# Third token tile from the transposed copy of x, its statistics through DRAM; tiles 4 and 5 split one tile sooner

## The chip, the core and the metric

The kernel runs on one core of a Trainium2 chip. The metric is the time on the device in microseconds (us), the median of several runs; lower is better. The engines are PE (matrix multiplication, with PEld for its weight loads), DVE, ACT and POOL (elementwise work, each strictly in the order of its own instruction list) and SP (here only a queue that issues DMAs and waits for semaphores).

## What is computed

One layer over 2048 tokens of width 640, all in float32. With xn the layer norm of x over its last axis:

```
q, k, v = split(xn @ wqkv)                      # 32 heads of 20
phi(u)  = [softmax(u @ w_phi), softmax(-(u @ w_phi))]   # per head, 40 features
kv, z   = sum over tokens of phi(k)^T v, of phi(k)
s       = (phi(q) kv / (phi(q) z + 1e-6)) @ wo
h       = gelu(xn @ w1 + b1);  g = silu(h @ w2 + b2)    # inner width 1536
out     = x + s * g
```

## The kernel before, in words

The tokens are 16 tiles of 128 (t = 0 to 15); two neighbours t = 2q and 2q + 1 make a pair q, with o = t % 2. The host hands over x twice: row by row (`x`) and transposed (`xt_in`). Every matmul in full precision is three matmuls in a faster format: each operand is split into a high part (a copy in that format, on ACT) and a low part (operand minus high part, on DVE or POOL), and `PASSES` (line 386) lists high x high, high x low, low x high.

**Start (to about 12 us).** PE folds w_phi into the key weights (`fold_w`, line 169), which gives `wk_s`, five pieces of 128 rows of the contraction.

**Keys and values, the stage of the change (about 12 to 150 us).** For each tile PE does `project(t, wk_s)` (line 388, 30 matmuls at line 397) and `value(t)` (line 451, 30 more). The keys go through `feat1` (maximum over a head, subtraction, minimum on DVE at lines 409 to 415; then the negative half on POOL, line 416), `feat2` (exponential on ACT, line 425) and `key_fin` (sums over a head and reciprocal on DVE, lines 433 and 465; scaling on POOL, line 438). `kv_pair(t)` (line 483) then adds the products of two tiles to one PSUM bank on PE (line 477); it follows the key projection of every odd tile from t = 3 on and takes tiles t - 3 and t - 2. Results of PE for one tile lie in `bankA`, three PSUM buffers in rotation. For tiles 4 to 7 `fold_pair` (line 180) also prepares query weights in such buffers, read by DVE at lines 187 and 188.

**How a tile of x becomes PE's stationary operand.** Both ways need the normalized x with the contraction on the partitions, split by `plain` (line 268; ACT at line 272, DVE at 274).
- By transposes (tiles 0, 1 and 2): `norm_a` or `stats` (line 215) take mean and variance per token on DVE, POOL raises the variance to the power -1/2 (line 223), DVE or ACT normalizes the tile (`norm_b`, `norm_act`), and `transpose_x` (line 377) does five PE transposes into PSUM, from which `plain` splits.
- From the transposed copy (tile 3 alone, then the pairs from 4 and 5 on): the statistics lie along partitions, but are now wanted along the free axis of all 128 partitions. So mean and power are stored to DRAM (`st_dram`), and a second DMA reads them back for every partition (`bc`). SP issues the store once POOL's power is there (lines 361, 322), and the broadcast when the store has landed (lines 363, 324). POOL then subtracts the mean (`one_sub`, line 370; for a pair `pair_sub`, two instructions at line 331), DVE multiplies (`one_plain`, line 374; `pair_mul`, line 336), and `plain` splits from SBUF. `one_load` (line 342) and `load_xr` (line 248) fetch the transposed x.

**What sets the order.** The whole start stage and the key stage are scheduled by hand: every engine, SP included, runs its instructions in the order in which the program issues them (`startup`, line 542). An instruction that waits holds up all that is behind it on its engine. Buffers for rows of x, raw weights, broadcasts and value rows come from one pool of eleven (`rows`), which is why the loads of tiles 6 and 7 wait on SP for tiles 0 and 1 to be done with. The lines around the change are 546 to 636: on POOL the order there is the low parts of the value weights (`split_v`, line 139), the negative half of tile 1's keys (416), `one_sub(3)` (370), the powers of tiles 4 and 5 (223), the scaling of tiles 0 and 1 (438), and, in the turn of tile 2, its negative half and `pair_sub(2)` (331).

**Pairs and the rest (from about 150 us).** Later tiles are handled in pairs with fewer multiplications by sums and differences of halves; then the feed-forward layers (lines 987 and 1016, about 237 to 550 us) and the attention output with the gate (line 1218, to the end).

Of the kernel before, what the change touches and what calls it, by code (L numbers as in the profile page):

```python
# [46 lines left out]
def hedgehog_gated_mlp_kernel(ctx: ExitStack, tc: tile.TileContext, x, xt_in, wqk, bd, wv, wo, w1, b1, w2, b2, out_t):  # L47
    nc = tc.nc
# [67 lines left out]
    b1t = const.tile([P, NF], F32, name="b1t")  # L116
# [34 lines left out]
    def load_fold(which, engs):  # L151
        tl = folds[:, which]
        for c, eng in enumerate(engs):
            if c == 1 and which:
                x_in(0, nc.scalar)
            eng.dma_start(tl[:, c], wqk[which, c, :, :6 * P].rearrange("p (i t) -> p i t", i=6))
        return tl
# [72 lines left out]
    def norm_a(t):  # L230
        sm = small.tile([P, 16], F32, tag="st", name="st")
        nrm[t] = sm, stats(t, sm, None, sm[:, 14:15])
# [6 lines left out]
    def norm_act(t):  # L239
        sm, xt = nrm.pop(t)  # L240
        nc.vector.tensor_scalar(sm[:, 15:16], sm[:, 12:13], -1.0, sm[:, 14:15], op0=OP.mult, op1=OP.mult)
        nc.scalar.activation(xt[:], xt[:], AF.Identity, bias=sm[:, 15:16], scale=sm[:, 14:15])
        xns[t] = xt
# [4 lines left out]
    def load_xr(q):  # L248
        h, p = divmod(q, SLOTS)
        xr = slab(F32, "xr", (P, KC, W2))[:]  # L250
        src = xt_in.rearrange("(k p) (h o q t) -> p k h o q t", p=P, h=NH, o=2, q=SLOTS)[:, :, h, :, p]
        nc.sync.dma_start(xr[:, :, :P], src[:, :, 0])
        nc.sync.dma_start(xr[:, :, P:], src[:, :, 1])
        xrs[q] = xr
# [13 lines left out]
    def plain(q, o, v, only=slice(0, 2), hi=True, lo=None):  # L268
        parts = [(xp[:, 0:5, :, at(q)], v)] if o == 0 else [(beside(q), v[:, 0:2]), (xp[:, 5:8, :, at(q)], v[:, 2:5])]
        parts = parts[only]  # L270
        for dst, src in parts if hi else ():
            nc.scalar.activation(dst[:, :, 0, :], src, AF.Copy)
        for dst, src in parts if lo is None else ():
            nc.vector.tensor_tensor(dst[:, :, 1, :], src, dst[:, :, 0, :].bitcast(F32), op=OP.subtract)
        for dst, src in parts if lo else ():
            nc.gpsimd.tensor_tensor(dst[:, :, 1, :], src, dst[:, :, 0, :].bitcast(F32), op=OP.subtract)
# [38 lines left out]
    def pair_stats(t):  # L315
        if t % 2 == 0:
            pst[0] = small.tile([P, 2, 2], F32, tag="pst", name="pst")
        sm = small.tile([P, 16], F32, tag="st", name="st")
        stats(t, sm, pst[0][:, t % 2, 0:1], pst[0][:, t % 2, 1:2])
        if t % 2:  # L320
            q = t // 2
            nc.sync.dma_start(st_dram[q].rearrange("i p s -> p i s"), pst[0][:])
            bc = row([P, W2, 2], F32, "bc")
            nc.sync.dma_start(bc[:].rearrange("p t s -> p (t s)"),
                              st_dram[q].rearrange("i p s -> (i p s)").partition_broadcast(P))
            pld[q] = bc

    def pair_sub(q):
        bc, xr = pld[q], xrs[q]
        for o in (slice(0, P), slice(P, W2)):  # L330
            nc.gpsimd.tensor_tensor(xr[:, :, o], xr[:, :, o], bc[:, None, o, 0].to_broadcast([P, KC, P]),
                                    op=OP.subtract)
# [9 lines left out]
    def one_load(t):  # L342
        q = t // 2
        h, p = divmod(q, SLOTS)
        xr = slab(F32, "xr", (P, KC, W2))[:]
        src = xt_in.rearrange("(k p) (h o q t) -> p k h o q t", p=P, h=NH, o=2, q=SLOTS)[:, :, h, t % 2, p]
        nc.sync.dma_start(xr[:, :, :P], src)
        xrs[t, "one"] = xr[:, :, :P]

    def one_stats(t):  # L350
        sm = small.tile([P, 16], F32, tag="st", name="st")
        ps = sm[:, 14:16]
        xt, st = xts.pop(t), sm[:, :12]
        for i in range(2):
            nc.vector.bn_stats(st[:, 6 * i:6 * i + 6], xt[:, i * HALF:(i + 1) * HALF])
        yield
        nc.vector.bn_aggr(sm[:, 12:14], st.rearrange("p (a b) -> p a b", a=2))
        nc.vector.tensor_scalar(ps[:, 1:2], sm[:, 13:14], LN_EPS, None, op0=OP.add)
        nc.gpsimd.tensor_tensor(ps[:, 1:2], ps[:, 1:2], mhalf[:], op=OP.pow)
        nc.vector.tensor_copy(ps[:, 0:1], sm[:, 12:13])  # L360
        nc.sync.dma_start(st_dram[t // 2, t % 2], ps)
        bc = row([P, P, 2], F32, "bc")
        nc.sync.dma_start(bc[:].rearrange("p t s -> p (t s)"),
                          st_dram[t // 2, t % 2].rearrange("p s -> (p s)").partition_broadcast(P))
        pld[t, "one"] = bc
        yield

    def one_sub(t):
        bc, xr = pld[t, "one"], xrs[t, "one"]
        nc.gpsimd.tensor_tensor(xr, xr, bc[:, None, :, 0].to_broadcast([P, KC, P]), op=OP.subtract)  # L370

    def one_plain(t):
        bc, xr = pld.pop((t, "one")), xrs.pop((t, "one"))
        nc.vector.tensor_tensor(xr, xr, bc[:, None, :, 1].to_broadcast([P, KC, P]), op=OP.mult)
        plain(t // 2, t % 2, xr)

    def transpose_x(t):
        q, o = divmod(t, 2)
        xn = xns.pop(t)
        ps = bankA()  # L380
        flat = ps[:].rearrange("p a b -> p (a b)")
        for k in range(KC):
            nc.tensor.transpose(flat[:, k * P:(k + 1) * P], xn[:, k * P:(k + 1) * P], ident[:])  # L383
        plain(q, o, flat[:, :D].rearrange("p (k t) -> p k t", t=P))
# [3 lines left out]
    def project(t, ws, mid=None, at_k=3):  # L388
        q, o = divmod(t, 2)
        ps = bankA()  # L390
        n = 0
        for k in range(KC):
            if k == at_k and mid is not None:
                mid()
            for a, b in PASSES:
                for hf in range(2):
                    nc.tensor.matmul(ps[:, hf, :HALF], stat_x(q, o, k, a),  # L397
                                     ws[k][:, b, hf * HALF:(hf + 1) * HALF],
                                     start=n == 0, stop=n == 3 * KC - 1)
                n += 1  # L400
        return ps
# [22 lines left out]
    def feat2(ef):  # L424
        nc.scalar.activation(ef, ef, AF.Exp)  # L425
        return ef
# [24 lines left out]
    def value(t, mid=None):  # L451
        ps = project(t, wv_s, mid)
        v, v3 = value_row()
        nc.scalar.activation(v3[:, :, :DH].rearrange("p (a h) d -> p a h d", a=2), heads(ps), AF.Copy)
        return v
# [12 lines left out]
    def key_fin(ef):  # L468
        scale_heads(ef, key_sums(ef))
        return ef  # L470
# [62 lines left out]
    def x_in(t, eng=None):  # L533
        xts[t] = load_x(t, eng)
# [13 lines left out]
    wv_raw = [load_raw(wv[c * P:(c + 1) * P, :]) for c in range(KC)]  # L548
    for t in (3, 4, 5):
        x_in(t)  # L550
    x_in(6)
    x_in(7)
    nc.sync.dma_start(b1t[:], b1)
    nc.sync.dma_start(b2t[:], b2)
    wv_s = []

    def split_v(c):
        wv_s.append(split_w(wv_raw[c][:], "wv", "dve" if c == 3 else "pool"))
# [10 lines left out]
    norm_a(1)  # L569
    fold_w(wkT, range(4, KC), "wk", wk_s)  # L570
    norm_act(1)
    norm_a(2)
    st3 = one_stats(3)
    next(st3)
    split_v(0)
    one_load(3)
    kvp[0] = bankB("kv")
    pk = project(0, wk_s, lambda: transpose_x(1), 4)
    split_v(1)
    next(st3)  # L580
    load_xr(2)
    norm_act(2)
    split_v(2)
    es[0] = feat1(pk)
    split_v(3)
    pk = project(1, wk_s, lambda: transpose_x(2))
    split_v(4)
    feat2(es[0])
    es[1] = feat1(pk)
    one_sub(3)  # L590
    pair_stats(4)
    vs[0] = value(0)
    pair_stats(5)
    wqT = load_fold(0, (nc.sync,) * KC)
    x_in(8)
    x_in(9)
# [3 lines left out]
    one_plain(3)  # L600
    phis[0] = key_fin(es.pop(0))
    vs[1] = value(1)
    phis[1] = key_fin(es.pop(1))
    vf = [v_forms(0), v_forms(1)]
    for t in range(2, 6):
        pk = project(t, wk_s)
        if t % 2:
            kv_pair(t - 3)
        es[t] = feat1(pk)
        if t == 4:  # L610
            next(vf[0])
        if t == 2:
            pair_sub(2)
            pair_stats(6)
            pair_stats(7)
            pair_mul(2)
        if t == 3:
            pair_plain(2)
        if t > 3:
            pair_stats(t + 4)  # L620
        if t in (3, 4, 5):
            spill(t - 3)
        if t == 5:
            x_in(10)
        if t == 4:
            pair_sub(3)
            pair_mul(3)
        vs[t] = value(t)
        if t >= 4:
            fold_pair(t - 4)  # L630
        if t == 5:
            next(vf[0])
        feat2(es[t])
        if t == 4:
            pair_plain(3)
        phis[t] = key_fin(es.pop(t))
# [200 lines left out]
    for p in range(5, 8):  # L837
        t = 2 * p
# [781 lines left out]
```

## Time and profile before

| what | value |
|---|---|
| median of 3 runs | 639.14 us (639.01 to 639.66) |
| the profiled execution | 637.78 us |
| its span, first to last instruction | 636.1 us |
| PE busy | 631.3 us, 99% |
| POOL busy | 432.5 us, 68% |
| DVE busy | 511.1 us, 80% |
| granted PE clock | 1.0 |

All rows come from the one profiled execution. In a timeline a row reads: start in us from the span's start, duration, engine, line, operation, output<-inputs, shape, count, and in brackets how long the engine sat idle before it and what ended that. Durations of neighbouring PE rows overlap; what a step takes is seen from one start to the next. A row of waits reads: who <- whom: us in total, times, longest. A row of a window reads: from:to, length, then busy us and count of PE, PEld, DVE, ACT and POOL, granted clock, share of the DMA engines, GB/s.

### The profile page before, as it was taken

The page shows a single profiled execution, that of the slowest core. Times are in us where ns is not written, and L with a number is a line of the kernel's source. Part 1 is how long each engine was busy: PE and PEld are TensorE (multiplying, and loading weights), DVE is VectorE, ACT ScalarE, POOL GpSimd, SP SyncE. Part 2 cuts the span into 40 slices and gives each one's busy share as a digit, 9 for nine tenths or more (in the row PEclk, how much of TensorE's full clock was granted, in tenths as well). Part 3 has the DMA queues.
Part 4 walks back from the last instruction along what each step waited for, and adds up shares of the span by engine and source line. Part 5 has one row for each costly group of instructions (what it writes and reads, how often), then busy time and mean ns, then how long its engine had stood idle before and what let it go on. Part 6 is the DMA issues. An engine that isn't in the chain of part 4 may idle for free.

```text
span 636.1 us, 11441 instructions
## 1 busy us (share of the span) xinstructions
PE 631.3 (99%) x4324; PEld 550.3 (87%) x4324; DVE 511.1 (80%) x790; ACT 259.7 (41%) x390; POOL 432.5 (68%) x376
## 2 busy tenths in 40 slices
PE   9999999999999999999999999999999999999997
PEld 9999999999999998888888888888888888667676
DVE  5887976789887877878979869758798899887586
ACT  3522422334344347243442534842322335455540
POOL 1877466888978857687878876381735678866363
PEclk9999999999999999999999999999999999999999
DMA  9577287393421488359899699697498598969934
GB/s 347 121 227 230 75 286 223 100 344 134 90 76 42 131 304 284 111 106 349 212 287 315 162 385 350 135 319 258 138 245 168 172 176 271 306 181 310 377 110 152
DMA packets 167168, 136.90 MB, mean 215 GB/s; under 512 B 89864, under 2 KB 130824, under 8 KB 166728
## 3 DMA queue, kind: packets, MB, share of 16 engines
q1 hardware_dynamic: 164376, 124.56, 65.9%
q10 hardware_dynamic: 2736, 11.60, 4.7%
q8 instruction: 34, 0.56, 0.4%
q14 instruction: 22, 0.18, 0.1%
HBM read 87.76 MB, written 48.38 MB: 214 GB/s over the span
## 4 chain that ended last, share of the span: by engine, by line
PE 98%; DMA 1%; DVE 0%; SPq 0%; issue 0%
PE pB L1016 26%; PE pB L987 23%; PE pA L397 22%; PE pB L1218 10%; PE pA L710 7%; PE pB L1144 3%; PE pA L164 2%; PE qV L710 2%; PE kv L477 2%; PE qY L710 1%; DMA folds<-in_wqk_dram 1%; PE pB L1126 0%; PE pA L383 0%; DVE y L1228 0%; PE pB L942 0%; DVE xres L1229 0%
## 5 line engine op out<-in xcount | busy, mean ns | idle before, releaser
L1016 PE MATMUL pB<-hs,w2s 128*128 128x512 f32 x720 | 165.9, 389 | 0.0
L1016 PEld LDWEIGHTS pB<-hs,w2s 128*128 128x128 f32 x720 | 135.0, 188 | 28.8 <-issue 0.8
L987 PE MATMUL pB<-xp,w1s 128*128 128x512 f32 x324 | 81.4, 389 | 0.0
L987 PE MATMUL pB<-xd,w1s 128*128 128x512 f32 x324 | 79.3, 389 | 0.0
L438 POOL TENSOR_TENSOR eq<-eq,rc 128x1280 f32<-128x1280 f32 x16 | 37.9, 2371 | 60.6 <-DVE rc L1078 48.4
L987 PEld LDWEIGHTS pB<-xp,w1s 128*128 128x128 f32 x324 | 60.7, 188 | 12.8 <-ACT x L1003 0.3
L987 PEld LDWEIGHTS pB<-xd,w1s 128*128 128x128 f32 x324 | 60.8, 188 | 12.6
L1025 DVE TENSOR_TENSOR y<-pB,y 128x512 f32<-128x512 f32 x100 | 63.1, 675 | 1.8 <-PE pB L1016 1.8
L992 ACT ACTIVATE pB<-pB,b1t 128x512 f32<-128x512 f32 x48 | 31.8, 662 | 77.3 <-DVE pB L1418 29.5
L397 PE MATMUL pA<-wk,xp 128*128 128x320 f32 x384 | 59.6, 310 | 0.0
L425 ACT ACTIVATE e<-e 128x1280 f32<-128x1280 f32 x32 | 40.7, 1271 | 43.3 <-POOL e L416 42.8
L397 PEld LDWEIGHTS pA<-wk,xp 128*128 128x128 f32 x384 | 56.9, 188 | 0.1
L416 POOL TENSOR_TENSOR e<-nr,e 128x640 f32<-128x640 f32 x32 | 44.8, 1402 | 15.9 <-DVE nr L415 15.5
L438 POOL TENSOR_TENSOR e<-e,rc 128x1280 f32<-128x1280 f32 x16 | 38.4, 2407 | 21.0 <-DVE rc L465 21.0
L1065 POOL TENSOR_TENSOR ez<-eq,zrep 128x1280 f32<-128x1280 f32 x16 | 47.4, 2962 | 2.8 <-DMA eq<-e_dram 2.8
L505 POOL TENSOR_TENSOR w1s<-raw,w1s 128x640 fp32r<-128x640 f32 (+1 forms) x18 | 25.4, 1410 | 18.0 <-ACT w1s L504 17.7
L139 POOL TENSOR_TENSOR w2s<-raw,w2s 128x640 fp32r<-128x640 f32 x23 | 36.1, 1589 | 0.2 <-ACT w2s L137 0.2
L998 DVE TENSOR_TENSOR hs<-pB,hs 128x512 fp32r<-128x512 f32 x48 | 32.0, 683 | 3.8 <-ACT hs L994 3.6
L137 ACT ACTIVATE w2s<-raw 128x640 fp32r<-128x640 f32 x24 | 17.2, 735 | 41.5 <-DVE dn L433 12.1
L409 DVE TENSOR_REDUCE mx<-pA 128x32 f32<-128x640 f32 x32 | 25.9, 809 | 8.9 <-PE pA L397 8.6
L994 ACT ACTIVATE hs<-pB 128x512 fp32r<-128x512 f32 x48 | 28.8, 600 | 2.1
L397 PE MATMUL pA<-wq,xp 128*128 128x320 f32 x192 | 29.6, 309 | 0.0
(220 smaller groups left out, 1281.0 us busy)
## 6 DMA issues: line engine op xcount, KB each, us to landing
raw<-in_w_dram SPq DMA_DIRECT2D x42, 320.0 KB
e_dram<-e ACTq DMA_DIRECT2D x16, 640.0 KB
eq<-e_dram SPq DMA_DIRECT2D x16, 640.0 KB
phi_t<-eq SPq DMA_DIRECT2D x64, 160.0 KB
phT<-phi_t SPq DMA_DIRECT2D x20, 512.0 KB
xt<-in_x_dram SPq DMA_DIRECT2D x16, 320.0 KB
xres<-in_xt_dram SPq DMA_DIRECT2D x20, 256.0 KB
out_dram<-xres SPq DMA_DIRECT2D x19, 256.0 KB
```

The lines of the kernel that those rows point to most:

```text
L139: eng.tensor_tensor(sl[:, 1, :], raw, sl[:, 0, :].bitcast(F32), op=OP.subtract)
L397: nc.tensor.matmul(ps[:, hf, :HALF], stat_x(q, o, k, a), ws[k][:, b, hf * HALF:(hf + 1) * HALF], start=n == 0, stop=n == 3 * KC - 1)
L416: rest = lambda: nc.gpsimd.tensor_tensor(e5[:, :, :, 1, :], nr[:, :, :, None].to_broadcast([P, 2, 16, DH]), e5[:, :, :, 0, :], op=OP.subtract)
L425: nc.scalar.activation(ef, ef, AF.Exp)
L438: nc.gpsimd.tensor_tensor(e3, e3, rc[:, :, None].to_broadcast([P, 64, DH]), op=OP.mult)
L710: nc.tensor.matmul(bank[ch], q_x(blk, a, q), p_weight(base, f, w, k)[:, b], start=ch not in seen and n == 0, stop=n == len(mms) - 1, skip_ ...
L987: nc.tensor.matmul(bank[ch][:], tl[:, a, off + wo_:off + wo_ + P], mov(blk, b), start=new and n == 0, stop=n == len(mms) - 1, skip_group_c ...
L998: nc.vector.tensor_tensor(hs[:, 1], ps, hs[:, 0].bitcast(F32), op=OP.subtract)
L1016: nc.tensor.matmul(ps[:], ws[i][:, b, d * P:(d + 1) * P], hs[o][i][:, a, :], start=i == n == 0, stop=(i, n) == (GF - 1, 2), skip_group_che ...
L1025: nc.vector.tensor_tensor(y, ps[:], y, op=OP.add)
L1065: nc.gpsimd.tensor_tensor(zv, ef, zf, op=OP.mult)
L1218: nc.tensor.matmul(ps[:, mv], w, o[:, mv], start=first and n == 0, stop=last and n == len(steps) - 1, skip_group_check=True)
```

## The change

Tile 2 leaves the way by transposes and takes tile 3's. `one_stats(2)` stores its statistics and broadcasts them (directly ahead of the first half of `one_stats(3)`), `one_load(2)` fetches its transposed x (ahead of the rows of tiles 6 and 7), `one_sub(2)` stands on POOL between the last value weights and the negative half of tile 1's keys, `one_mul(2)` on DVE between the statistics of tiles 4 and 5. `norm_act(2)`, and `transpose_x(2)` within the key projection of tile 1, are gone. The two bias loads move behind tile 3's broadcast on SP. For the pair of tiles 4 and 5, `pair_sub(2)` moves ahead of `key_fin` of tile 1 on POOL, and `pair_plain(2)` from the turn of tile 3 to that of tile 2.

```diff
--- before.py
+++ after.py
@@ -369,10 +369,13 @@
         bc, xr = pld[t, "one"], xrs[t, "one"]
         nc.gpsimd.tensor_tensor(xr, xr, bc[:, None, :, 0].to_broadcast([P, KC, P]), op=OP.subtract)
 
-    def one_plain(t):
+    def one_mul(t):
         bc, xr = pld.pop((t, "one")), xrs.pop((t, "one"))
         nc.vector.tensor_tensor(xr, xr, bc[:, None, :, 1].to_broadcast([P, KC, P]), op=OP.mult)
-        plain(t // 2, t % 2, xr)
+        return xr
+
+    def one_plain(t):
+        plain(t // 2, t % 2, one_mul(t))
 
     def transpose_x(t):
         q, o = divmod(t, 2)
@@ -548,10 +551,9 @@
     wv_raw = [load_raw(wv[c * P:(c + 1) * P, :]) for c in range(KC)]
     for t in (3, 4, 5):
         x_in(t)
+    one_load(2)
     x_in(6)
     x_in(7)
-    nc.sync.dma_start(b1t[:], b1)
-    nc.sync.dma_start(b2t[:], b2)
     wv_s = []
 
     def split_v(c):
@@ -569,28 +571,34 @@
     norm_a(1)
     fold_w(wkT, range(4, KC), "wk", wk_s)
     norm_act(1)
-    norm_a(2)
+    for _ in one_stats(2):
+        pass
     st3 = one_stats(3)
     next(st3)
+    one_load(3)
     split_v(0)
-    one_load(3)
     kvp[0] = bankB("kv")
     pk = project(0, wk_s, lambda: transpose_x(1), 4)
     split_v(1)
     next(st3)
+    nc.sync.dma_start(b1t[:], b1)
+    nc.sync.dma_start(b2t[:], b2)
     load_xr(2)
-    norm_act(2)
     split_v(2)
     es[0] = feat1(pk)
     split_v(3)
-    pk = project(1, wk_s, lambda: transpose_x(2))
+    pk = project(1, wk_s)
     split_v(4)
+    one_sub(2)
     feat2(es[0])
     es[1] = feat1(pk)
     one_sub(3)
     pair_stats(4)
+    x2 = one_mul(2)
     vs[0] = value(0)
+    plain(1, 0, x2, lo=False)
     pair_stats(5)
+    plain(1, 0, x2, hi=False)
     wqT = load_fold(0, (nc.sync,) * KC)
     x_in(8)
     x_in(9)
@@ -600,6 +608,7 @@
     one_plain(3)
     phis[0] = key_fin(es.pop(0))
     vs[1] = value(1)
+    pair_sub(2)
     phis[1] = key_fin(es.pop(1))
     vf = [v_forms(0), v_forms(1)]
     for t in range(2, 6):
@@ -610,11 +619,9 @@
         if t == 4:
             next(vf[0])
         if t == 2:
-            pair_sub(2)
             pair_stats(6)
             pair_stats(7)
             pair_mul(2)
-        if t == 3:
             pair_plain(2)
         if t > 3:
             pair_stats(t + 4)
```

## Prediction

> **What bounds the kernel now.** I read the page first: engines, then the chain that ended last.
>
> ```profile
> PE 631.3 (99%) x4324; PEld 550.3 (87%) x4324; DVE 511.1 (80%) x790; ACT 259.7 (41%) x390; POOL 432.5 (68%) x376
> PE 98%; DMA 1%; DVE 0%; SPq 0%; issue 0%
> PE pA L541 <- PEq L1610: 0.8, 1, 0.8
> PE pA L164 <- DMA folds<-in_wqk_dram: 0.2, 1, 0.2
> ```
>
> The last two lines are the whole list of waits of the PE. After 7.9 us it waits for nothing until its last matmul. So an instruction taken from the PE is worth its slot, and any new wait of the PE, however early, is added in full, since no later idle time can take it back. The question is how much cover each input of the PE has. I read that from the timelines of PE, SP and POOL up to 70 us.
>
> **What is taken from the PE.** The timeline of the PE around the five transposes of tile 2 and the steps behind them:
>
> ```profile
> 20.49 0.71 PE L383 MATMUL pA<-ident,xt 128*128 128x128 f32 x5
> 20.95 2.00 PE L397 MATMUL pA<-wk,xp 128*128 128x320 f32 x12
> 22.79 4.56 PE L397 MATMUL pA<-wv,xp 128*128 128x320 f32 x30
> 27.19 1.92 PE L397 MATMUL pA<-wv,b 128*128 128x320 f32 x12
> 31.59 4.56 PE L397 MATMUL pA<-wk,xp 128*128 128x320 f32 x30
> 44.88 1.37 PE L477 MATMUL kv<-e,v 128*32 128x40 f32 x128
> 46.19 2.02 PE L397 MATMUL pA<-wv,b 128*128 128x320 f32 x12
> 66.65 1.39 PE L477 MATMUL kv<-e,v 128*32 128x40 f32 x128
> 67.97 2.02 PE L397 MATMUL pA<-wv,b 128*128 128x320 f32 x12
> L383 PE MATMUL pA<-ident,xt x15: 270/272/328, 10.6 to 20.9; 128*128 128x128 f32 x15
> ```
>
> Undisturbed, 30 projection matmuls take 27.19 - 22.79 = 4.40 us, 0.147 each. The transposes take 20.95 - 20.49 = 0.46 us from start to start, and the 12 matmuls behind them 1.84 instead of 1.76, so 0.08 for the change of kind. The removal is worth 0.54 us, and everything behind it on the PE is due 0.54 us earlier: the projection of tile 2 at 31.05, the kv products of tiles 0 and 1 at 44.34 and, half of 46.19 - 44.88 later, those of tile 1 at 45.0 (before 45.54).
>
> The mean of one transpose in the last row, 272 ns, would give 1.36 us, but the transposes overlap. The Trainium skill (TensorE: Matmul & The Clock Gate, Part 4: PE-mode transpose) gives about 275 ns for a transpose in one kernel's context; five would give 1.4 us, and the sum would come out 0.8 us lower. The trace agrees with the duration and not with its use as a price.
>
> ACT loses one normalization and two copies' work of tile 2 becomes a copy from SBUF; DVE gains a multiplication. Neither engine sets an end here, except as said below.
>
> **What is added: a round trip through DRAM, ahead of another one.** Tile 3 makes this trip already, and tiles 4 and 5 a second one. SP's and POOL's timelines have all their steps:
>
> ```profile
> 9.21 8.20 SPq L132 DMA_DIRECT2D xt<-in_x_dram  x5
> 20.77 0.34 SPq L361 DMA_DIRECT2D st_dram<-st  x1
> 23.94 0.33 SPq L363 DMA_DIRECT2D bc<-st_dram  x1
> 24.32 0.43 SPq L252 DMA_DIRECT2D xr<-in_xt_dram  x1
> 31.69 0.37 SPq L322 DMA_DIRECT2D st_dram<-pst  x1
> 34.94 0.34 SPq L324 DMA_DIRECT2D bc<-st_dram  x1
> 35.33 2.86 SPq L156 DMA_DIRECT2D folds<-in_wqk_dram  x5
> 16.61 0.55 POOL L223 TENSOR_TENSOR st<-st,mhalf 128x1 f32<-128x1 f32 x1 [1.62 <-DVE st L222]
> 24.25 1.57 POOL L139 TENSOR_TENSOR wv<-raw,wv 128x640 fp32r<-128x640 f32 x1
> 26.41 1.28 POOL L416 TENSOR_TENSOR e<-nr,e 128x640 f32<-128x640 f32 x1 [0.59 <-DVE nr L415]
> 28.80 1.59 POOL L370 TENSOR_TENSOR xr<-xr,bc 128x640 f32<-128x640 f32 x1 [1.12 <-DMA bc<-st_dram]
> 37.28 2.37 POOL L438 TENSOR_TENSOR e<-e,rc 128x1280 f32<-128x1280 f32 x1
> 40.84 3.15 POOL L331 TENSOR_TENSOR xr<-xr,bc 128x640 f32<-128x640 f32 x2
> ```
>
> SP stands still between a store of statistics and the broadcast that reads it: 23.94 - 20.77 = 3.17 us, and 34.94 - 31.69 = 3.25 for the pair. From the issue of a 128 KB broadcast to POOL's use of it pass 28.80 - 23.94 = 4.86 us. In the new order SP issues store 2, broadcast 2, the xr load of tile 3, store 3, broadcast 3, and only then the loads of pair 2; the pair's store waits for POOL, and POOL's list has the subtraction of tile 3 ahead of the pair's statistics.
>
> Is the second trip served beside the first, or behind it? Three rows, the first the rate in 40 slices from 24.3 to 30.5 us, the others windows (the last column is GB/s):
>
> ```profile
> GB/s 0 0 0 0 0 40 7 26 33 0 0 0 0 0 0 0 0 79 132 99 109 145 182 215 264 317 344 340 353 353 340 340 291 268 221 221 211 241 59 0
> 34.90:39.10 4.20, 4.20 (x31) 4.20 (x30) 4.10 (x6) 0.00 (x0) 4.20 (x4) 1.00 0.50 60
> 39.10:45.00 5.90, 5.90 (x52) 5.71 (x55) 3.33 (x11) 1.87 (x2) 5.90 (x6) 1.00 1.02 407
> ```
>
> First bytes come 1.1 us after the broadcast's issue, then almost none until 26.9, though 640 KB of xr loads stood issued behind it from 24.32 on. Over 34.90 to 39.10 move 60 x 4.2 = 252 KB, which is the pair's 256 KB broadcast alone, while fold loads issued from 35.33 wait. So a broadcast holds up what is queued behind it, for about 4.2 us from its issue. The Trainium skill (DMA: Bandwidth & Descriptors, Queues, rings and completion order) says the same: an engine consumes the descriptors of one ring in order.
>
> Now the sum in absolute times. Store 2 is ready when POOL's power ends (17.16) and SP is past the fifth x load (17.41), so 17.45; 320 KB of that load, 0.8 us at 407 GB/s, stand ahead of it, so its wait is 3.2 to 4.2, I take 4.0. **T = 21.4** (20.4 to 21.7) for broadcast 2.
> Tile 2: subtraction on POOL at T + 4.86 = 26.3, when POOL is through with the last wv part (before: 25.8), until 27.9; the exponent's partner of tile 1 (L416) follows until 29.2, before it ended at 27.7.
> Tile 3: its store, issued at T + 0.85, moves when broadcast 2 and the 320 KB load (at the 340 GB/s of the first row) have passed, T + 4.2 + 1.0; behind the bytes lies 3.2 - 1.1 = 2.1. Broadcast 3 goes at T + 7.3 = 28.7 (T + 4.05 if nothing queues), and the subtraction of tile 3 starts at 28.7 + 4.86 = **33.6** instead of 28.80.
> Pair 2: from that subtraction to the pair's store were 31.69 - 28.80 = 2.89 us, so the store goes at 36.5, the broadcast at 39.7, and it is there at 39.7 + 4.86 to 5.4 (it has twice the bytes; I take 5.2) = 44.9. Its subtractions take 3.1 us, to 48.0.
> The change puts these subtractions ahead of the scaling of tile 1's features (L438) on POOL; that scaling takes 2.37 and ends at **50.4**. Before, it ended at 39.65, and its cover until the PE used it was 45.5 - 39.65 = 5.9 us. The PE wants it at 45.0, so it stands still for **5.4 us**.
>
> **What is late next.** Behind the stall PE and POOL start together, at E = 50.4. In the trace of before the PE takes 67.97 - 45.54 = 22.4 us from the kv products of tile 1 to the values of tile 5, which take over a PSUM bank that DVE's folded-query work (L188) must have read.
>
> ```profile
> 45.43 1.48 DVE L433 TENSOR_REDUCE rc<-e 128x64 f32<-128x1280 f32 x1
> 49.81 0.89 DVE L274 TENSOR_TENSOR xp<-xr,xp 128x640 fp32r<-128x640 f32 x1
> 51.87 1.27 ACT L425 ACTIVATE e<-e 128x1280 f32<-128x1280 f32 x1 [0.28 <-POOL e L416]
> 53.17 1.49 DVE L433 TENSOR_REDUCE rc<-e 128x64 f32<-128x1280 f32 x1 [0.59 <-ACT e L425]
> 66.86 0.49 DVE L188 TENSOR_TENSOR sr<-sr,pA 128x320 f32<-128x320 f32 x1
> 30.43 0.82 DVE L374 TENSOR_TENSOR xr<-xr,bc 128x640 f32<-128x640 f32 x1 [1.53 <-POOL xr L370]
> 45.55 0.74 ACT L272 ACTIVATE xp<-xr 128x640 fp32r<-128x640 f32 x1 [3.09 <-DVE xr L336]
> 0.84 4.18 PE L541 MATMUL pA<-const-float32-1.0 128*128 128x128 f32 x18 [0.84 <-PEq L1610]
> ```
>
> The other side of that bank: L416 and the exponent of tile 2 (1.28 + 1.27), sums and features (49.81 - 45.43 = 4.38), the same pair for tile 3 (2.55) make E + 9.5, and from the sums of tile 3 to the read of the bank were 67.35 - 53.17 = 14.2: E + 23.5 or so. That is **1.0 us** of a second wait.
> The split of tile 4, in the L274 row, was ready at 50.70, when the PE began tile 4 (50.68); the change takes it to 50.4 to 51.2, five microseconds ahead of the delayed use, so it gains nothing. The split of tile 2 gets ready at about 31.0: POOL to 27.9, the L374 kind 0.82, one statistics block of the pair on DVE ahead of the low half (about 1.3, beside ACT's 0.74), an L274 kind of 0.89. It is used at 31.05; were it late by some tenths, the stall at 45 would swallow that.
> The last row is a clock term: the first 18 matmuls of the kernel, after an idle PE, take 4.18 us, 0.22 apart, against 0.09 for transposes of the same shape. If 5.4 us of idle bring that state back, four microseconds at half rate cost up to 2.0 us, of which the second wait swallows 1.0. From nothing to 1.0; I take 0.5. The Trainium skill (TensorE: Matmul & The Clock Gate, Part 1) puts the loss of the clock at an idle window of some 3.4 us; by it the term would be full. No wait of that length stands in this trace.
>
> **Sum:** -0.54 + 5.4 + 1.0 + 0.5 = +6.4 us. The profiled execution has 637.78 us (span 636.1 and 1.7 around it), so 644.2 for one like it; it lies 1.36 below the median of the runs, 639.14, from which I forecast **645.5**.
>
> **Rivals.**
> *Trips side by side* (0.15). If store 3 does not queue, tile 3's subtraction starts at T + 4.05 + 4.86, 29.3 to 30.6, and the scaling ends 16.8 later, at 46.1 to 47.4: stalls of 1.1 to 2.4 and of 1.0, less 0.54, +1.6 to +2.9, which is 640.7 to 642.0. Against it speak the rate rows above.
> *No stall* (0.13). If the trips are so short that the scaling of tile 1 ends by 45.0, 5.4 us sooner than in my sum, only the gain is left: -0.54, 638.6. It is the one that decides the other way, from the point where the pair's broadcast is there by 39.5. For it: the cover of 5.9 us, and three stores and three broadcasts in a row in which an error adds up. Against it: a store took 3.17 and 3.25, a broadcast 4.86 on a queue with nothing ahead. The Trainium skill (DMA: Bandwidth & Descriptors, Anatomy of one DMA) has about 2 us plus the bytes at 436 GB/s; by it store and broadcast would take 2.0 and 2.3 us and this rival would hold. The trace differs on both.
> *Longer* (0.07). A third late resource, such as later wq folds behind the later broadcast of the pair, takes it past +8.5.
> The forecast has 0.65. Its own range: T from 20.4 to 21.7, broadcast of the pair 4.86 to 5.4, clock term 0 to 1.0: +4.5 to +7.4, and with 1 us more on the second wait +8.4.
>
> A measurement of this kernel tells about 0.2% (1.3 us) from no change. Faster by more than that needs over twice the removed PE time: 0.03. The no-stall case falls within: 0.13. The rest, 0.84, is slower. The range runs from the side-by-side case to the forecast's upper end: 640.4 to 647.6.
>
> **What would show it.** Waits of the PE: a new line at L477 on POOL of about 5.4 us, and one of about 1 us at L397 on DVE near 75 us. POOL: L370 twice, the second near 33.6 waiting for the broadcast, and L331 near 45 waiting likewise, ahead of a L438. SP: two waits of 3 to 7 us at L363. Right in kind but not in size, if L477 waits 1 to 2 us. Wrong, if L477 does not wait, or if the PE waits first for tile 2's split.

## The result, and the profile after

The changed kernel takes 648.99 us (median of 4 runs, 648.88 to 651.01), the kernel before 639.18 us beside it (639.01 to 639.66): a ratio of 1.0161, 95% interval 1.0146 to 1.0176. It is 9.8 us slower. The prediction had slower, by 6.4 us, and the time lies above its range. The profiled execution is the longest of the four (651.01 us, span 649.3); of the others there is no trace. The lines of the changed file are 3 higher than before from `project` on: 397 has become 400, 416 is 419, 425 is 428, 433 is 436, 438 is 441, 477 is 480; in some of the runs below a line stands a little further on (L401 or L421 for L400, L442 for L441, L718 for L717). One run of all, 708.65 us at a granted clock of 0.85, in the first filling of the long wait, is left out of the numbers below.

First the page's engine line and its chain of work that ended last, then the list of the PE's waits (without those of the first microseconds and one of 0.2):

```profile
PE 633.7 (98%) x4319; PEld 551.8 (85%) x4319; DVE 516.7 (80%) x791; ACT 259.2 (40%) x389; POOL 434.3 (67%) x377
PE 74%; POOL 7%; DVE 7%; DMA 6%; issue 2%; ACT 1%; SPq 1%; ACTq 0%; POOLq 0%; DVEq 0%
```

```profile
PE kv L480 <- POOL e L441: 6.1, 1, 6.1
PE pA L717 <- DVE e L415: 1.7, 1, 1.7
PE pA L400 <- ACT xp L272: 1.4, 1, 1.4
...
PE pA L717 <- DVE v L731: 0.8, 1, 0.8
```

The chain that was 98% PE now runs through the other engines for a quarter of the span: up to the last of these waits the PE no longer sets the pace. The timeline of the PE shows where it falls behind:

```profile
44.86 0.80 PE L480 MATMUL kv<-e,v 128*32 128x40 f32 x64
51.74 1.29 PE L480 MATMUL kv<-e,v 128*32 128x40 f32 x64 [6.08 <-POOL e L441]
52.96 3.36 PE L400 MATMUL pA<-wv,b 128*128 128x320 f32 x12
74.76 1.39 PE L480 MATMUL kv<-e,v 128*32 128x40 f32 x128
77.55 2.00 PE L400 MATMUL pA<-wv,b 128*128 128x320 f32 x12 [1.40 <-ACT xp L272]
161.76 1.12 PE L717 MATMUL pA<-wv,xp 128*128 128x320 f32 x6 [1.72 <-DVE e L415]
```

Against the rows of before (44.88, 66.65, 67.97, and 45.54 for the second half of the kv products) the PE is level at 44.86, 6.2 us late at 51.74, 8.1 late at 74.76 and 9.6 late at 77.55. The rest of the 13.2 us between the spans, 3.6, falls behind that. "Level" hides a gain: this execution began its folds 0.4 us later.

Now the way of the statistics, on SP and on POOL:

```profile
17.62 0.33 SPq L361 DMA_DIRECT2D st_dram<-st  x1
21.84 0.33 SPq L363 DMA_DIRECT2D bc<-st_dram  x1
...
22.75 0.46 SPq L361 DMA_DIRECT2D st_dram<-st  x1
29.00 0.32 SPq L363 DMA_DIRECT2D bc<-st_dram  x1
...
37.06 0.37 SPq L322 DMA_DIRECT2D st_dram<-pst  x1
41.03 0.34 SPq L324 DMA_DIRECT2D bc<-st_dram  x1
```

```profile
26.46 1.59 POOL L370 TENSOR_TENSOR xr<-xr,bc 128x640 f32<-128x640 f32 x1 [0.36 <-DMA bc<-st_dram]
...
34.18 1.59 POOL L370 TENSOR_TENSOR xr<-xr,bc 128x640 f32<-128x640 f32 x1 [4.89 <-DMA bc<-st_dram]
...
46.31 3.06 POOL L331 TENSOR_TENSOR xr<-xr,bc 128x640 f32<-128x640 f32 x2 [3.60 <-DMA bc<-st_dram]
49.33 2.36 POOL L441 TENSOR_TENSOR e<-e,rc 128x1280 f32<-128x1280 f32 x1
51.64 2.52 POOL L419 TENSOR_TENSOR e<-nr,e 128x640 f32<-128x640 f32 x1
```

Store 2 takes 4.2 us to its broadcast, store 3 takes 6.25, the pair's 3.97. POOL stands still for 4.89 us before tile 3 and 3.60 before the pair, then scales tile 1's features until 51.69, and the PE's kv products start.

What follows the scaling, on DVE and ACT, is the place where the forecast went short:

```profile
49.40 3.63 DVE L336 TENSOR_TENSOR xr<-xr,bc 128x1280 f32<-128x1280 f32 x1 [2.44 <-POOL xr L331]
56.30 1.49 DVE L436 TENSOR_REDUCE rc<-e 128x64 f32<-128x1280 f32 x1 [0.65 <-ACT e L428]
...
76.92 0.49 DVE L188 TENSOR_TENSOR sr<-sr,pA 128x320 f32<-128x320 f32 x1
```

```profile
53.06 0.74 ACT L272 ACTIVATE xp<-xr 128x640 fp32r<-128x640 f32 x1 [14.98 <-DVE xr L336]
...
55.01 1.26 ACT L428 ACTIVATE e<-e 128x1280 f32<-128x1280 f32 x1
```

From the end of the scaling (51.69) to the sums of tile 2 (56.30) pass 4.61 us, where the prediction had 2.55. L419 takes 2.52 instead of 1.28, because POOL stands behind the pair's multiplication (L336), which began at 49.40, was itself held up by the scaling, and takes 3.63 instead of 1.49: 1.24 us. Then ACT has the pair's high parts (from 53.06) ahead of tile 2's exponential, which starts at 55.01, about 0.8 after POOL's end at 54.16: together 2.05. These causes are read from the times of the rows. From the sums on to the values of tile 5 it is 77.55 - 56.30 = 21.25 us. The row of that wait names ACT's L272, the last to end before it. But the PSUM bank that the values of tile 5 take over is the one that L188 must have read, and that read ends at 77.41.

Last the clock, in three windows that follow the long wait (the third column from the right is the granted clock):

```profile
45.70:51.70 6.00, 0.00 (x0) 0.00 (x0) 3.49 (x6) 0.00 (x0) 5.39 (x4) 0.78 1.03 407
51.70:55.90 4.20, 4.16 (x75) 4.08 (x76) 3.14 (x4) 2.84 (x5) 4.20 (x3) 0.50 1.03 314
55.90:60.00 4.10, 4.10 (x30) 4.10 (x29) 3.59 (x5) 1.08 (x2) 1.78 (x4) 1.00 0.09 9
```

The PE works its first 4.2 us after the wait at half its clock, and loses 8.1 - 6.2 = 1.9 us by it.

### The profile page after: what moved, and what is told of

The parts are those of the page before. It is cut to its first block, busy times and chain, and to the rows that moved or that the text cites. A ratio compares the mean times of both kernels' runs of the same rounds, so it can differ in the third digit from the quotient of the medians.

```text
span 649.3 us, 11437 instructions
## 1 busy us (share of the span) xinstructions
PE 633.7 (98%) x4319; PEld 551.8 (85%) x4319; DVE 516.7 (80%) x791; ACT 259.2 (40%) x389; POOL 434.3 (67%) x377
## 4 chain that ended last, share of the span: by engine, by line
PE 74%; POOL 7%; DVE 7%; DMA 6%; issue 2%; ACT 1%; SPq 1%; ACTq 0%; POOLq 0%; DVEq 0%
PE pB L1023 25%; PE pB L994 23%; PE pB L1225 10%; PE pA L717 7%; PE pB L1151 3%; PE pA L400 3%; DMA bc<-st_dram 2%; DMA xt<-in_x_dram 2%; POOL e L419 2%; PE qV L717 1%; POOL e L441 1%; DMA st_dram<-pst 1%; PE qY L717 1%; DVE rc L436 1%; POOL xr L331 1%
## 5 line engine op out<-in xcount | busy, mean ns | idle before, releaser
L441 POOL TENSOR_TENSOR eq<-eq,rc 128x1280 f32<-128x1280 f32 x16 | 37.9, 2371 | 59.9 <-DVE rc L1085 42.7
L400 PE MATMUL pA<-wk,xp 128*128 128x320 f32 x384 | 59.5, 310 | 0.0
L400 PEld LDWEIGHTS pA<-wk,xp 128*128 128x128 f32 x384 | 56.9, 188 | 0.2
L419 POOL TENSOR_TENSOR e<-nr,e 128x640 f32<-128x640 f32 x32 | 44.2, 1384 | 16.4 <-DVE nr L418 13.1
L441 POOL TENSOR_TENSOR e<-e,rc 128x1280 f32<-128x1280 f32 x16 | 37.8, 2368 | 21.0 <-DVE rc L468 21.0
L412 DVE TENSOR_REDUCE mx<-pA 128x32 f32<-128x640 f32 x32 | 25.8, 807 | 7.6 <-PE pA L400 7.3
L400 PE MATMUL pA<-wq,xp 128*128 128x320 f32 x192 | 29.6, 310 | 0.2 <-DVE e L415 0.2
```

The lines of the kernel that those rows point to most:

```text
L400: nc.tensor.matmul(ps[:, hf, :HALF], stat_x(q, o, k, a), ws[k][:, b, hf * HALF:(hf + 1) * HALF], start=n == 0, stop=n == 3 * KC - 1)
L419: rest = lambda: nc.gpsimd.tensor_tensor(e5[:, :, :, 1, :], nr[:, :, :, None].to_broadcast([P, 2, 16, DH]), e5[:, :, :, 0, :], op=OP.subtract)
L441: nc.gpsimd.tensor_tensor(e3, e3, rc[:, :, None].to_broadcast([P, 64, DH]), op=OP.mult)
```

## The experiments

The theory: the price is a chain, not one wait. (a) Two trips through DRAM in a row bring tile 3's subtraction, and behind it the pair's, about 5 us later. (b) As the pair's subtraction now stands ahead of the scaling of tile 1, the scaling ends at E = 51.7. (c) The values of tile 5 come 25.9 us after E, whatever the PE does. (d) A wait of the PE of more than some 2 us costs it the clock as well. The rivals: the trips do not queue; the moved pair costs nothing by itself; the slow clock is a cost of its own that the later wait doesn't swallow.

### The trip alone

The changed kernel with the pair's work where it was before:

```diff
     vs[1] = value(1)
-    pair_sub(2)
     phis[1] = key_fin(es.pop(1))
...
         if t == 2:
+            pair_sub(2)
             pair_stats(6)
             pair_stats(7)
             pair_mul(2)
+        if t == 3:
             pair_plain(2)
```

> The changed kernel with the subtractions and the split of tiles 4 and 5 back in their old places; tile 2's trip through DRAM stays. Theory (two serial trips make the pair's broadcast late, whatever the order on POOL): the broadcast is there at about 45.5 us, so POOL subtracts until 48.6, DVE multiplies until 50.1, and with sums (2.0) and features (2.4) ahead of it the low part of tile 4 is ready near 55.3, where PE wants it at 50.1. A wait of about 5.2 us moves from the kv products to the key projection of tile 4: 643.8 us if the clock stays, up to 645.7 if the slow state costs 1.9 on the path; no wait at the kv products. Rival (the moved subtraction alone makes the loss, the trips only use idle time): near 638.6, no wait over 0.5 us.

Measured: 644.98 us (643.96 to 647.44) against 638.31, ratio 1.0107 (1.0088 to 1.0126). The first waits of its PE:

```profile
PE pA L400 <- DVE xp L274: 3.5, 1, 3.5
PE pA L718 <- DVE e L415: 1.3, 1, 1.3
```

There is no wait at the kv products. The late trip shows at the next user instead, the split of tile 4, with 3.5 us where the theory had 5.2: the PE first does four matmuls that need only the high part. The clock is at half for 6.8 us, from 53.35 on, within this wait. So the trip, in this order on SP, costs some 6.7 us by itself, and the PE waits for the pair wherever its work stands.

### The order alone

The kernel before, tile 2 by transposes, with only the pair's work moved:

```diff
     vs[1] = value(1)
+    pair_sub(2)
     phis[1] = key_fin(es.pop(1))
...
         if t == 2:
-            pair_sub(2)
             pair_stats(6)
             pair_stats(7)
             pair_mul(2)
-        if t == 3:
             pair_plain(2)
```

> The kernel before with only the second part of the change: the pair's subtractions ahead of tile 1's scaling, its split in the turn of tile 2; tile 2 keeps its transposes. The broadcast is there at about 40.2 us, the scaling ends near 45.7, PE wants it at 45.5: a wait of 0.2 us at the kv products. Theory (what follows the scaling sets the time: in the changed kernel PE could start the values of tile 5 25.9 us after the scaling's end, because the exponential of tile 2 stands behind the pair's high parts on ACT, and these behind a DVE multiplication that takes 3.6 us beside POOL's work): a wait of 3 us or more at the values of tile 5, 642.2 us. Rival (the chain as I had added it up, 23.5 us): a wait of 1.2 us, 640.5. Second rival (the order is free by itself): 639.2.

Measured: 648.53 us (645.43 to 649.52), ratio 1.0144 (1.0119 to 1.0169).

```profile
PE pA L397 <- ACT xp L272: 3.3, 1, 3.3
PE pB L986 <- DVE e L412: 2.7, 1, 2.7
```

```profile
42.90 2.36 POOL L438 TENSOR_TENSOR e<-e,rc 128x1280 f32<-128x1280 f32 x1
...
71.41 3.54 PE L397 MATMUL pA<-wv,b 128*128 128x320 f32 x12 [3.34 <-ACT xp L272]
```

The scaling ends at E = 45.26, in time for the kv products, and no wait stands there. The values of tile 5 come at 71.41, 26.15 after E, and wait 3.3 us; the PE then runs at half clock. A further wait of 2.7 at 247 us, also followed by half clock, was expected by no theory. Of the 10.7 us between the spans, 3.4 are the wait at tile 5, 2.6 the slow clock behind it, and 4.5 the wait at 247 us with its slow clock, whose cause stays open. The five runs lie 4 us apart, and the shortest has a mean clock of 1.0, so the slow stretches do not come every time. The moved pair is no neutral reordering: without any added trip it costs some 6 us by the chain and its clock, and with the unexplained wait about as much as the whole change. The two parts do not add up in time (6.7 and 10.2 alone, 9.8 together). At the values of tile 5 they nearly do: the PE is late there by 6.2 and 3.4 us alone, and by 9.6 and 8.0 in the two profiles of the changed kernel.

### The split of the pair one turn later

The changed kernel, but with the pair's high and low parts back in tile 3's turn; its subtraction stays early:

```diff
             pair_mul(2)
+        if t == 3:
             pair_plain(2)
```

> The changed kernel with only the pair's split (ACT's high parts, DVE's low parts) back in the turn of tile 3; the subtractions stay ahead of tile 1's scaling. The exponential of tile 2 then no longer stands behind the high parts on ACT: it can go when POOL ends tile 2's negative half (54.1 us in the profile after) instead of 55.0. Theory (the chain behind the scaling sets the time): 0.8 us or somewhat more off the wait at the values of tile 5, 648.0 us; the wait of 6 us at the kv products stays. Rival (the stall at the kv products and the clock alone set the time): unchanged, 648.9, or longer, as the low part of tile 4 gets late.

Measured: 647.05 us (645.77 to 648.4), ratio 1.0134 (1.012 to 1.0148).

```profile
PE kv L480 <- POOL e L441: 5.3, 1, 5.3
...
PE pA L400 <- DVE xp L274: 0.6, 1, 0.6
```

The wait at tile 5 is gone; a shorter one at tile 4's split takes its place. With the high parts out of the way on ACT the sums of tile 2 start at 54.31, 3.8 us after the scaling's end at 50.49 and not 4.6: the 0.8 us are those of the order on ACT. The other 1.24 us stay, since L336 and L419 collide here too (3.63 and 2.52 us). At tile 5, however, nothing is gained:

```profile
76.42 2.02 PE L400 MATMUL pA<-wv,b 128*128 128x320 f32 x12
```

That is 25.93 us after the scaling's end, against 25.86 in the changed kernel. The PE is held up by the wait for tile 4's split, and the read of the bank (L188) ends at 75.88, 25.39 after the scaling against 25.72, so of the 0.8 us only 0.3 are left there. That this run is shorter than the changed kernel has other sources: by the profiles the scaling ended 1.2 us sooner, and behind tile 5 the PE lost 1.2 us and not 3.6. The theory's saving at tile 5 is not shown: early or late, the split leaves the values of tile 5 where they are.

### Filling the long wait

Constant matmuls, whose result nothing reads, between the kv products of tiles 0 and 1 of the changed kernel. They are fp32 and take two passes each, which was overlooked the first time: 50 of them took 11.43 us and not half of it.

```diff
+            if u == 1:
+                pw = bankB("warm")
+                for i in range(50):
+                    nc.tensor.matmul(pw[:, :P], one, one, start=True, stop=True)
```

> The changed kernel with 50 extra matmuls on PE, 128x128 on constants into an unused PSUM bank, between the kv products of tile 0 and tile 1, where PE stands still; they take about 5.5 of the 6.1 us. Theory: the slow clock after the standstill (1.9 us of slower matmuls in the profile after) is hidden, since PE waits 1.4 us for DVE at the values of tile 5 afterwards anyway. With the extra matmuls the slow stretch goes, that wait grows from 1.4 to about 3.3, and the time stays within 0.3 us of the changed kernel's. Rival (the clock loss lies on the path): 1.9 us less, 647.1. Third possibility (the matmuls are slow for another reason than the idle PE): the kv products and tile 3's values stay slow, no change.

Measured: 650.13 us (649.67 to 650.45), ratio 1.0181 (1.0167 to 1.0195). The fill ended at 56.87, 7.4 us after the scaling (49.46 in this run), so it had itself become what is late. Behind it the clock stayed at 1.0 and the values of tile 5 did not wait. It tells that the slow clock comes from the idling, but not what it costs. So once more, with 25:

> The changed kernel with 25 fp32 matmuls of constants (two passes of 0.114 us each, 5.7 us in all) between the kv products of tiles 0 and 1, where the PE stands still for 6.1 us; their result is used by nothing. Theory (the chain behind the scaling on POOL sets the values of tile 5, 25.9 us later, whatever the PE does): kv products of tile 1 again near 51.7, the clock no longer drops, the PE reaches the values of tile 5 some 1.8 us earlier and waits there 3.2 us instead of 1.4: the total does not change against the changed kernel. Rival (the slow clock is a cost of its own): 1.8 us less than the changed kernel.

Measured: 651.1 us (647.75 to 651.49), ratio 1.0181 (1.0159 to 1.0204). Rows of the PE's timeline, then two windows:

```profile
45.16 5.85 PE L491 MATMUL warm<-const-float32-1.0 128*128 128x128 f32 x50
50.94 0.80 PE L480 MATMUL kv<-e,v 128*32 128x40 f32 x64
...
76.47 3.43 PE L400 MATMUL pA<-wv,b 128*128 128x320 f32 x12 [2.94 <-ACT xp L272]
```

```profile
51.00:55.00 4.00, 4.00 (x88) 3.95 (x87) 2.79 (x4) 3.00 (x5) 4.00 (x4) 1.00 0.97 291
76.40:79.80 3.40, 3.33 (x13) 3.35 (x14) 3.39 (x5) 0.72 (x3) 0.00 (x0) 0.52 0.49 193
```

The clock holds behind the kv products, the PE is in front of the values of tile 5 earlier, and it gains nothing: the wait there grows to 2.94 us, and tile 5 comes at 76.47, 25.8 us after the scaling's end at 50.63. The rival, 1.8 us less, is out. The longer wait then brings the half clock itself. The profiled run took 648.66 us, as long as the changed kernel; three of the five took 651.1 to 651.5, 2 us more than the theory allows, and of these there is no trace.

### Store 3 ahead of broadcast 2

The changed kernel; the generator of the statistics gets one more stop, so that the load for tile 3 and store 3 are issued before broadcast 2:

```diff
         nc.sync.dma_start(st_dram[t // 2, t % 2], ps)
+        yield
         bc = row([P, P, 2], F32, "bc")
...
-    for _ in one_stats(2):
-        pass
+    st2 = one_stats(2)
+    next(st2)
+    next(st2)
...
     next(st3)
+    next(st2)
+    next(st3)
```

> The changed kernel, with one step moved: SP issues the load of tile 3's transposed rows and the store of tile 3's statistics before it issues broadcast 2, so that store 3 no longer stands behind broadcast 2. If the second trip queues behind the first (theory), tile 3's subtraction on POOL starts near 29.7 us instead of 34.2, the pair's broadcast lands some 4 us sooner, the scaling of tile 1's features ends near 47 instead of 51.7, the wait at the kv products is 1 to 2 us instead of 6.1, the PE's clock stays at 1.0, and the values of tile 5 (25.9 us behind the scaling) come near 73: about 4.5 to 5 us over the kernel before. Rival (the trips never queued, tile 3's subtraction was late for another reason): no change against the changed kernel, some 10 us over the kernel before.

Measured: 646.35 us (646.14 to 646.78) against 638.21, ratio 1.0124 (1.0106 to 1.0143). POOL's and the PE's rows:

```profile
31.44 1.57 POOL L371 TENSOR_TENSOR xr<-xr,bc 128x640 f32<-128x640 f32 x1 [1.67 <-DMA bc<-st_dram]
...
46.72 2.36 POOL L442 TENSOR_TENSOR e<-e,rc 128x1280 f32<-128x1280 f32 x1
```

```profile
PE pA L401 <- ACT xp L272: 3.2, 1, 3.2
PE kv L481 <- POOL e L442: 1.8, 1, 1.8
PE pA L401 <- DVE xp L274: 1.5, 1, 1.5
```

Tile 3's subtraction starts at 31.44: 2.7 us sooner than at 34.18, but not the 4.5 of the theory. Store 3 took 5.4 us even ahead of broadcast 2 (4.4 in the next run), so the queueing explains only part of its length; why it is so long is left open. Later steps go as the theory says: the wait at the kv products falls to 1.8, and the values of tile 5 come at 74.90, 25.8 us after the scaling's end at 49.08. But there the PE waits 3.2 us, and 3.4 us at half clock follow, which cost 1.5 us; the theory had the clock at 1.0. The 1.5 us at tile 2's split, from the later broadcast 2, were not expected either. The total is 8.1 us over the kernel before, not the expected 4.5 to 5.

### The same, with the pair's work in its old places

The edits of the last run and of the first together.

> As the run above (store 3 ahead of broadcast 2), and the pair's subtraction, multiplication and split put back where the kernel before has them, behind the scaling of tile 1 and in the turn of tile 3. What is left of the change is tile 2 without transposes, its trip beside tile 3's. Theory: no wait at the kv products of tile 1; the split of tile 4 follows tile 3's subtraction, which is about 1 us later than before (29.7 against 28.8), so a wait of 1 to 1.6 us at tile 4's key projection, less 0.5 us for the transposes; no drop of the clock after so short a wait: +0.5 to +1.1 us against the kernel before, inside what can be told from no change. Rival (a trip through DRAM for tile 2 costs much wherever it stands): a wait of 3 us or more at tile 4, as in the run where only the trip was added.

Measured: 639.87 us (12 runs, 638.94 to 641.54), ratio 1.0025 (1.0013 to 1.0037). Its longest wait:

```profile
PE pA L401 <- DVE xp L274: 1.9, 2, 1.2
```

The waits are where the theory has them, 1.2 us at tile 4, none at the kv products or at tile 5, and no slow clock. Another 0.7 at tile 2's split, from the later broadcast 2, were not expected, so the total is 1.7 us over the kernel before and not 0.5 to 1.1. Tile 3's subtraction starts at 30.42. The rival, 3 us or more at tile 4, is out: a trip for tile 2 is not that dear wherever it stands.

### Two tries to beat both kernels

Tile 3's power and store ahead of POOL's first value weights, in the last kernel:

```diff
     st3 = one_stats(3)
     next(st3)
+    next(st3)
     one_load(3)
     split_v(0)
...
     split_v(1)
-    next(st3)
     next(st2)
```

> As the run with store 3 ahead of broadcast 2 and the pair's work in its old places, and tile 3's statistics (its power on POOL and its store) put ahead of POOL's first two wv parts: store 3 goes near 18.8 us instead of 21.1, broadcast 3 about 2 us sooner, tile 3's subtraction near 28.7, as early as in the kernel before. Theory (what is left of the slowdown is the 0.7 us at tile 2's split and the 1.2 us at tile 4's, both from the late second trip and from POOL and DVE in each other's way): no wait at tile 4, at most 0.3 us at tile 2, PE 0.2 to 0.5 us earlier than before: 637.7 to 638.2, not to be told from the kernel before. Rival (two trips in a row always hold each other up): a wait of 1 us or more stays at tile 4's key projection.

Measured: 639.73 us (12 runs, 639.31 to 642.77) against 638.16, ratio 1.0028 (1.0014 to 1.0043). And one store and one 256 KB broadcast for both tiles, in a new generator that takes the place of the two:

```diff
...
+        nc.sync.dma_start(st_dram[1].rearrange("i p s -> p i s"), ps[:])
+        yield
+        bc = row([P, W2, 2], F32, "bc")
+        nc.sync.dma_start(bc[:].rearrange("p t s -> p (t s)"),
+                          st_dram[1].rearrange("i p s -> (i p s)").partition_broadcast(P))
+        for t in (2, 3):
+            pld[t, "one"] = bc[:, (t - 2) * P:(t - 1) * P]
...
```

> Old places for the pair's work, and one trip for tiles 2 and 3 together: one store of both tiles' statistics and one broadcast of 256 KB, instead of two of each. Theory (a trip costs its round time, hardly its bytes): store near 18.6, broadcast near 22.5, there near 27.5; tile 2's subtraction then instead of 26, so its split is 1 to 1.5 us late for its key projection, and tile 3's subtraction near 30; no wait at tile 4 above 0.5 us: PE +0.5 to +1 us. Rival (queueing of the second trip is nothing, only the number of steps counts): the same as with two trips, +1.7.

Measured: 640.46 us (12 runs, 639.74 to 641.65), ratio 1.0033 (1.002 to 1.0045). The PE's waits for a split are one of 0.8 us with the early store, and two of 1.4 us together with one trip.

Neither beats the kernel before, and neither met its theory in full. The early store leaves 0.8 us at tile 4: POOL's subtraction of tile 3 starts at 29.40 but takes 2.20 us instead of 1.59, and the pair's store goes at 33.47 against 31.69 before. One trip for both makes tile 2 late, as expected, but by 0.6 us only, and leaves 0.8 at tile 4, where at most 0.5 was expected; its rival, the same as with two trips, fits the time better. The 0.54 us of the transposes is less than these waits in each of the three kernels (0.8 to 1.9 us).

### The changed kernel once more

> The changed kernel again, unaltered, for its waits in a second profile. Theory: the waits of 6.1 us at the kv products and of 1.4 us at the values of tile 5 come again to 0.3 us, as does the slow clock between 49 and 56 us. Not settled: the waits at 157 to 170 us (1.7 and 0.8 us), where POOL and DVE want to read SBUF at the same time; if they are a matter of which of the two starts first by a few hundredths of a microsecond, they may be absent, and the time 2 us less.

Measured: 648.87 us (647.57 to 649.69), ratio 1.0161 (1.0142 to 1.018); profiled execution 649.5, span 647.8.

```profile
PE kv L480 <- POOL e L441: 5.0, 1, 5.0
PE pA L717 <- DVE e L415: 2.1, 1, 2.1
PE pA L400 <- ACT xp L272: 1.7, 1, 1.7
PE pA L717 <- DVE v L731: 0.8, 1, 0.8
```

Both waits of the key stage come again. The first is 1.1 us shorter, where the theory had it equal to 0.3, mainly since store 3 took 5.4 us and not 6.25; the slow stretch behind it is 3.4 us long and not 6.8. The values of tile 5 come 25.8 us after the scaling. The waits at 157 to 170 us stand here too, so they belong to the cost in both profiles of the changed kernel. What precedes them, in the first profile, and the same two instructions in the run with store 3 ahead:

```profile
156.43 3.59 DVE L655 TENSOR_TENSOR ws<-raw,ws 128x640 fp32r<-128x640 f32 x1
...
156.97 2.37 POOL L441 TENSOR_TENSOR e<-e,rc 128x1280 f32<-128x1280 f32 x1
```

```profile
153.95 1.20 DVE L659 TENSOR_TENSOR ws<-raw,ws 128x640 fp32r<-128x640 f32 x1
...
154.42 2.95 POOL L442 TENSOR_TENSOR e<-e,rc 128x1280 f32<-128x1280 f32 x1
```

DVE and POOL both stand ready behind a POOL subtraction (L331). Where POOL goes on first, DVE loses 2.4 us; where DVE goes first, POOL loses 0.6. POOL went first in both profiles of the changed kernel and in the one with the trip alone, all with a wait of 1.3 to 2.1 us behind it, and in none of the others. The later wait, of 0.8 us, stands also where DVE went first (the run with the split one turn later). That this causes the wait of 1.3 to 2.1 us is read from the order of the rows; no run took the collision away, and what decides who goes first stays open.

## Why the prediction was right in direction and short in size

| term, us | predicted | first profile | second profile |
|---|---|---|---|
| start of the folds and transposes gone | -0.54 | 0.0 | -0.4 |
| stall at the kv products of tile 1 | 5.4 | 6.2 | 5.1 |
| slow clock behind it | 0 to 1.0, taken 0.5 | 1.9 | 1.6 |
| wait at the values of tile 5 | 1.0 | 1.5 | 1.7 |
| everything later | 0 | 3.6 | 3.7 |
| sum, as the difference of the spans | 6.4 | 13.2 | 11.7 |

The columns are made from starts of the PE's rows against those of before, and against the profiled execution of before, which lies 1.36 us under its median; by medians the change costs 9.8 and, the second time, 10.7 us.

**Right:** the transposes' worth. From 44.88 to 44.86 lie a later start of 0.4 and a gain of about 0.5. The route: SP's two waits at the broadcasts, POOL's list, the pair's subtraction ahead of the scaling. The steps came at 21.84 (predicted 21.4), 34.18 (33.6), 37.06 (36.5), 41.03 (39.7) and the end of the scaling at 51.69 (50.4). Of the 1.3 us that it ended too late, 0.4 are the later start; the rest is the pair's store, 3.97 us instead of 3.25, and small change. That the earlier split gains nothing was right as well, and tile 2's split was in time.

**Wrong, the first step that failed:** "E + 23.5 or so. That is 1.0 us of a second wait", in "What is late next". Its own terms, 9.5 and 14.2, add up to 23.7, and 1.2 us of wait. It is E + 25.8 to 26.2 in all five traces in which this chain sets the values of tile 5. The prediction took L416 and the exponential of tile 2 undisturbed, at 1.28 + 1.27. It left out that the change itself puts two things in their way: the pair's multiplication on DVE, against POOL, and the pair's high parts ahead of the exponential on ACT. It had counted where the moved split becomes ready, but not who is queued behind it, although the order of ACT's list told it. By the rows the two are worth 1.24 and 0.8 us. The split put back took the 0.8 from ACT but brought tile 5 no sooner, and no run took the collision on DVE away: the length of the chain is shown, its division into these two is not. The run with the order alone shows that the moved pair is enough for a wait of 3.3 us with no added trip at all.

**Mis-sized:** the clock. The forecast took half of a term of up to 2.0 as swallowed by the second wait. Its size was right (1.9), but the second wait, being longer by 2.3 us, stayed above it. In this chain the clock costs nothing: filled with matmuls, tile 5 still comes at E + 25.8. The table's 1.9 and 1.5 are one sum, the length of the chain, 25.8, less the 22.4 us that the PE needs at full clock: 3.4. Of what the forecast lacked, 1.9 us are this chain.

**Missing:** anything behind 78 us. The rival "Longer" named a third late resource, with 0.07 and a wrong candidate (the folds of the query weights). By the first profile 3.1 of the 3.6 us fall at two waits for DVE, at 160 and 169 us; the medians leave room for less, and only for the first of the two do the rows suggest a cause.

**The rivals:** side by side and no stall are both refuted by the trace; store 3 took 6.25 and 5.4 us. But of the 4.5 us that the experiment's theory put down to queueing, putting store 3 first gained 2.7, and 3.8 with the pair's work in its old places. (What the rival without a stall draws on in the Trainium skill, DMA: Bandwidth & Descriptors, Anatomy of one DMA, is a fit for DMAs issued from POOL; these are issued by SP.) Two lower ends are off by about 0.3 from their own terms, without weight here: T (17.45 + 3.2 = 20.65, not 20.4) and the range (640.7, not 640.4).

## What to carry to other kernels

When an instruction is moved ahead on one engine, walk the chain on from it through every engine's list, and ask for each step who now stands in front of it: the second wait here came from sums and an exponential that the edit didn't mention. Where the PE never waits, 0.54 us taken from it are soon lost to a new wait, and the late step behind a wait of 5 us made another one 25 us later. Try the parts of a change one at a time: here each alone cost 6 us and more.

## What the runs showed of the hardware

Idling and the clock: waits of the PE of up to 2.1 us (1.4, 1.7, 1.8, 2.1) left the clock at 1.0; with every wait from 2.7 us on in these traces (2.7, 2.9, 3.2, 3.3, 3.5, 5.0 and longer) came a stretch of 3.4 or 6.8 us at 0.5, which began within the wait or up to 1.5 us behind it. The Trainium skill (TensorE: Matmul & The Clock Gate, Part 1) has one idle window of about 3.4 us as what brings the half clock. The lengths of the slow stretches agree with multiples of it; the wait that suffices was shorter here, 2.7 us.

DVE and POOL on SBUF: a DVE multiplication of two SBUF operands that takes 1.49 us alone took 3.63 beside two POOL instructions, and POOL's next took 2.52 instead of 1.28. The Trainium skill (SBUF — State Buffer, SBUF: two separate sides) describes an exclusive lock, taken for a whole instruction, with the other engine fully blocked. The rows agree: POOL's scaling ran its 2.36 us unhindered, DVE's multiplication ended about 1.3 us after it, and only then POOL's next ran its 1.28.

A 1 KB store to DRAM needed 3.2 us to its dependent broadcast in the kernel before, where one load stood ahead of it, 5.4 to 6.25 as the second of two behind a broadcast (six traces with the changed order on SP), and 5.4 and 4.4 as the second of two with no broadcast ahead of it.
